# A two-layer long-convolution and MLP kernel: k, v, q and the spectrum swap moved in 4 KB rows, k and v loaded ahead of the second-stage tables, a new list of priorities

## The chip, the cores and the metric

The kernel runs on one core of one Trainium2 chip. The metric is the time of one execution on the device in microseconds (us); the time before is the median of three runs. The core has five engines with a program each: PE (TensorE, matmuls), DVE (VectorE), ACT (ScalarE), POOL (GpSimd) and SP (SyncE), which here only issues DMAs. Data lies in SBUF (128 partitions); PE writes to PSUM, from where ACT or DVE must copy ("evacuate") a result before PE can use the place again.

## The reference

```python
def _A_ref(q, k, v, shift_k, ssm_k, ssm_D):      # (1, 2048, 512) each
    ...                                          # k_shift: 4-tap causal filter of k along the sequence
    kv = k_shift * v
    L = 2 * S
    ...
    kv_f = rfft(kv padded to L); kf_f = rfft(ssm_k padded to L)
    y = irfft(kv_f * kf_f)[:, :S]                # a causal convolution over the sequence
    y = y + kv * ssm_D
    return q * y

x = A_q
x = x + _A_ref(layernorm(x), k, v, shift_k, ssm_k, ssm_D)
x = x + _B_ref(layernorm(x), w1, b1, w2, b2)     # layernorm, 512 -> 1376, gelu, 1376 -> 512
x = x + _A_ref(layernorm(x), k, v, ...)          # the same convolution output y, with the new x as q
x = x + _B_ref(layernorm(x), w1, b1, w2, b2)
```

All tensors are bf16. The convolution's y depends on k, v and the weights alone, so the kernel computes it once and uses it in both layers.

## The kernel before, in words

The program is straight-line: no loop runs on the chip. Python code declares operations, each with the memory that it reads and writes, its engine (or a choice of ACT and DVE for evacuations) and a planned length. A planner (`Prog.schedule`) then deals the operations out to the engines. It takes at each step the operation that can start first and breaks ties by a priority: the length of the work that hangs on the operation, plus a number for the operation's group from the table `BIAS`; `SHY` holds back DVE from taking an evacuation that ACT would do faster. The result is one fixed list per engine. `Prog.sync` adds the semaphore waits, and every engine works through its list in order. DMAs get a priority by the order in which they are declared, so SP's list follows the code's order where the data allow it.

The work, with the group names of the tables:

- **Loads.** SP issues the filter `ssm_k` (4 DMAs of 512 KB), `shift_k`, then eight 512 KB pieces of the table `tab_s2` (`tload`, L506) for the second transform stage, then two small DMAs with the last rows of the neighbour's k ("halo"), then k (one DMA, 128 partitions with 16 KB each), v (the same), small tables, biases.
- **ht, h1, h2: the filter's spectrum H.** Transposes (PE, L563), first stage (`stage1`, PE L580, 16 pairs of weight load and matmul to a group, each group evacuated by ACT L514 or DVE L515), second stage (`stage2`, PE L593, 16 groups of 8 pairs; needs `tab_s2`).
- **The spectrum swap.** The upper and lower 64 partitions of H are copied crosswise into a second buffer HS by four SBUF-to-SBUF DMAs (L498, `ar<-ar`) of 64 partitions with 16 KB each: two for the first half of the channels, two for the second. They wait for the last h2 evacuation, since each h2 group writes a stripe of every channel.
- **fir0 to fir3: the 4-tap filter of k, times v.** Blocks 0 and 1 of 128 channels go over PE (transposes L622, matmuls with diagonal weights L634, evacuated by DVE times v, L641). Blocks 2 and 3 are done on DVE alone, eight operations on 128x2048 each (L509).
- **x1_0 to x1_3: first transform stage of k*v** (`stage1` again, PE L580, 64 pairs for a channel block).
- **x2, i1, i2.** For each half of the channels (`PARTS`): second stage (`products`, PE L680, 8 groups of 16 pairs), evacuation, a DVE product with H and HS (L509, 128x2048), the first inverse stage (`inverse1`, PE L704); then `inverse2` (PE L760). These evacuations take 128x1024 each, nearly all on ACT.
- **T2, W1, q, W2** are loaded into the places of k and v, so SP issues them after fir and behind the swap.
- **The layers.** q and z: layer norms and gates on DVE and POOL; m1 and m2: the MLP's two products (PE L860 and L879), with gelu on ACT (L865) and the residual sum on DVE (L883). Transposes go over PE (L847) for the first blocks and over DMA later.

A "pair" below is one weight load (PEld) with its matmul (PE); PE's list holds 2248 of them. Up to the stage x2 they are numbered by adding up the counts of PE's rows.

Of the kernel before, what the change touches and what calls it, by code (L numbers as in the profile page):

```python
# [12 lines left out]
PE, ACT, DVE, POOL, SP = "tensor", "scalar", "vector", "gpsimd", "sync"  # L13
# [31 lines left out]
class Prog:  # L45
# [3 lines left out]

    G = 4  # L50
    LAT = 130.0
    BIAS = {'fir0': 55600, 'fir1': 5900, 'fir2': 62400, 'fir3': -169800, 'h1': 26100, 'h2': 31300, 'ht': 93000, 'i1_0': -56100, 'i1_64': 19100, 'i2_0': -72300, 'i2_64': 146700, 'm1': 113300, 'm2': -28100, 'q0': -4600, 'q1': -11900, 'q2': 28400, 'q3': -9200, 'q5': -46400, 'q6': -62400, 'q7': -55200, 'x1_0': 12800, 'x1_1': -24600, 'x1_2': -100, 'x1_3': 12900, 'x2_0': 193200, 'x2_64': 7000, 'z0': 8600, 'z1': -14300, 'z2': -51600, 'z3': -4800, 'z5': 11600, 'z6': 8700, 'z7': 49400}
    SHY = {'fir0': 1000, 'fir1': 300, 'h1': 0, 'h2': 210, 'ht': 1000, 'i1_0': 1000, 'i1_64': 0, 'i2_0': 3000, 'i2_64': 1000, 'x1_0': 150, 'x1_1': 2600, 'x1_2': 300, 'x1_3': 300, 'x2_0': 150, 'x2_64': 0, 'z0': 150, 'z1': 600}

    def __init__(self, nc):
        self.nc = nc
# [124 lines left out]
    def schedule(self):  # L181
# [9 lines left out]
        for o in reversed(ops):  # L191
# [19 lines left out]
        while done < n:  # L211
            best = None
            for e in free:
                te = max(free[e], 0.0)
                cand = None
                for o in ready[e]:
# [6 lines left out]
                    if new:  # L223
# [210 lines left out]
def bass_interleave_layers__ssm_conv_h3__mixer_channel_mlp__prompt_kernel(  # L434
        nc, A_q, A_k, A_v, A_shift_k, A_ssm_k, A_ssm_D, B_x, B_w1, B_b1, B_w2, B_b2, out):
    P = Prog(nc)
# [5 lines left out]
    def A(p0, n, off, *dims):  # L442
        return bass.AP(ar, p0 * AR + off, [[AR, n]] + [list(d) for d in dims])
# [12 lines left out]
    def dr(t, off, *dims):  # L456
        return bass.AP(t.tensor, off, [list(d) for d in dims])
# [39 lines left out]
    def dma(dst, src, nbytes, reads=(), prio=0.0, writes=None, eng=SP, rate=400.0):  # L497
        return P.op(eng, lambda e: e.dma_start(dst, src, allow_slow_non_contiguous=True), 550.0, reads=reads,  # L498
                    writes=[dst] if writes is None else writes, dma=True, nbytes=nbytes * 370 / rate, prio=prio)

    U16 = mybir.dt.uint16

    def tload(t, row, off, dst_off, n, eng=SP, prio=0.0):
        dst = A(0, 128, dst_off, [1, n])
        src = bass.AP(t, off, [[row, 128], [1, n]])
        return P.op(eng, lambda e: e.dma_start(dst.bitcast(U16), src), 450.0, writes=[dst], dma=True, nbytes=256 * n * .925, prio=prio)  # L506
# [32 lines left out]
    dma(A(16, 112, R_K + c0, [512, 3], [1, WDV]),
        dr(A_k, (16 * 15 + 13) * 512 + c0, [16 * 512, 112], [512, 3], [1, WDV]), 112 * 6 * WDV, writes=halo[1:2])  # L540
    dma(A(1, 15, R_K + c0, [512, 3], [1, WDV]),
        dr(A_k, 13 * 512 + c0, [16 * 512, 15], [512, 3], [1, WDV]), 15 * 6 * WDV, writes=halo[2:])
# [234 lines left out]
    def stats(sl, double, gate=()):  # L777
# [35 lines left out]
    for L in range(2):  # L813
        s0 = 0
        for n in (BLOCKS0, BLOCKS1)[L]:
# [15 lines left out]
            k = blk[0] % 2  # L831
            blk[0] += 1
            for i, s in enumerate(sl):
                z = ntmp()
                norm(s, mr[i], A(0, 128, z, [1, 512]))
                dst = A(0, 128, R_XT + k * 2048 + i * 128, [512, 4], [1, 128])
                if L or s >= 4:
                    zs = A(0, 128, z, [1, 512])
                    P.op(SP, lambda e, zs=zs, dst=dst: e.dma_start_transpose(dst, zs), 1300.0, reads=[zs], writes=[dst],
                         dma=True, nbytes=1 << 17)  # L840
                    continue
                tl = Tile(ptr)
                src = [A(0, 128, z + 128 * j, [1, 128]) for j in range(4)]
# [8 lines left out]
            for fc in range(11):  # L852
# [5 lines left out]
                def f(e, ins=ins, tl=tl, rows=rows, w=w):  # L858
# [4 lines left out]
                dst = A(0, rows, R_HT + k * 5632 + fc * 512, [1, w])  # L863
# [3 lines left out]
                    reads=[bias], writes=[dst], tile=tl)  # L867
            for i, s in enumerate(sl):
# [7 lines left out]
                for lo, hi in ((0, 4), (4, 8), (8, 11)):  # L876
                    def f(e, ins=ins, tl=tl, lo=lo, hi=hi):
# [45 lines left out]
```

## Time and profile before

| what | value |
|---|---|
| measured, median of 3 | 259.44 us (258.97 to 259.62) |
| the profiled execution | 257.8 us; its span on the chip 256.0 us |
| granted TensorE clock, mean | 0.98 |
| PE busy | 226.3 us, 88% |
| DVE busy | 175.9 us, 69% |
| ACT busy | 137.4 us, 54% |
| DMA traffic | 27.63 MB, queue q1 27.21 MB, queue q8 (instructions) 17 packets, 0.28 MB |

In the profile, an engine is followed by the line of the program, the operation, what it writes and reads (`ar` is SBUF, `ps` PSUM), shapes and counts. q1 is the queue of SP's DMAs, q8 the queue over which the engines' own program code comes in. "issue" is time in which an engine waited for nothing that the profile shows. The chain of waits is followed back from the end of the program: at each step to the work that released it.

The profiled execution is 1.6 us shorter than the median; the prediction's sum is made against the profiled one and the difference carried over.

### The profile page before, as it was taken

The page shows a single profiled execution, that of the slowest core. Times are in us where ns is not written, and L with a number is a line of the kernel's source. Part 1 is how long each engine was busy: PE and PEld are TensorE (multiplying, and loading weights), DVE is VectorE, ACT ScalarE, POOL GpSimd, SP SyncE. Part 2 cuts the span into 40 slices and gives each one's busy share as a digit, 9 for nine tenths or more (in the row PEclk, how much of TensorE's full clock was granted, in tenths as well). Part 3 has the DMA queues.
Part 4 walks back from the last instruction along what each step waited for, and adds up shares of the span by engine and source line. Part 5 has one row for each costly group of instructions (what it writes and reads, how often), then busy time and mean ns, then how long its engine had stood idle before and what let it go on. Part 6 is the DMA issues. An engine that isn't in the chain of part 4 may idle for free.

```text
span 256.0 us, 5259 instructions
## 1 busy us (share of the span) xinstructions
PE 226.3 (88%) x2233; PEld 147.3 (58%) x2248; DVE 175.9 (69%) x358; ACT 137.4 (54%) x189; POOL 29.9 (12%) x58
## 2 busy tenths in 40 slices
PE   2977688484869997999999999999999999999994
PEld 2966587383769995767654444444444444444441
DVE  0887699952999988892999939789697662102223
ACT  2478779481999888855621824705507445173000
POOL 1410000000000204212030110130203010000000
PEclk9999999975899999999999999999999999999999
DMA  6999918998990000022021220140224213110112
GB/s 248 358 375 366 416 24 164 246 205 265 382 337 5 5 0 0 3 41 44 0 51 32 44 41 0 26 60 0 42 41 64 63 20 62 44 41 37 45 41 82
DMA packets 23367, 27.63 MB, mean 108 GB/s; under 512 B 17233, under 2 KB 19248, under 8 KB 22448
## 3 DMA queue, kind: packets, MB, share of 16 engines
q1 hardware_dynamic: 23198, 27.21, 36.6%
q8 instruction: 17, 0.28, 0.4%
q10 hardware_dynamic: 146, 0.10, 0.2%
q14 instruction: 6, 0.05, 0.1%
HBM read 17.34 MB, written 2.10 MB: 76 GB/s over the span
## 4 chain that ended last, share of the span: by engine, by line
PE 67%; DVE 11%; DMA 7%; ACT 6%; issue 4%; SPq 4%
PE ps L879 29%; PE ps L860 28%; DVE ar L509 8%; DMA ar<-in_A_k_dram 7%; PE ps L704 6%; ACT ar L514 4%; SPq L498 3%; PE ps L580 3%; ACT ar L865 2%; SPq L506 1%; DVE ar L641 1%; DVE ar L515 1%; PE ps L680 1%; DVE ar L883 1%; PE ps L760 0%
## 5 line engine op out<-in xcount | busy, mean ns | idle before, releaser
L865 ACT ACTIVATE ar<-ps,sm 128x512 bf16<-128x512 f32 (+3 forms) x110 | 63.4, 601 | 72.4 <-PE ps L860 51.4
L514 ACT ACTIVATE ar<-ps 128x1024 bf16<-128x1024 f32 (+2 forms) x76 | 71.9, 1046 | 24.9 <-PE ps L580 17.5
L860 PE MATMUL ps<-ar 128*128 128x512 bf16 (+3 forms) x435 | 77.9, 336 | 1.3 <-ACT ar L514 1.1
L879 PE MATMUL ps<-ar 128*128 128x512 bf16 (+1 forms) x342 | 76.7, 379 | 0.5
L860 PEld LDWEIGHTS ps<-ar 128*128 128x128 bf16 (+1 forms) x440 | 43.7, 100 | 34.6 <-ACT ar L514 1.2
L509 DVE TENSOR_TENSOR ar<-ar 128x512 bf16<-128x512 bf16 (+2 forms) x104 | 60.8, 642 | 3.0 <-DMA ar<-in_A_k_dram 2.1
L879 PEld LDWEIGHTS ps<-ar 128*128 128x128 bf16 (+1 forms) x352 | 34.3, 98 | 40.7
L883 DVE TENSOR_TENSOR ar<-ar,ps 128x512 bf16<-128x512 bf16 x32 | 21.1, 683 | 50.3 <-PE ps L879 50.3
L788 DVE BATCH_NORM_STATS2 sm<-ar 128x6 f32<-128x512 bf16 (+1 forms) x68 | 41.1, 644 | 0.0
L515 DVE CAST ar<-ps 128x1024 bf16<-128x1024 f32 x18 | 21.3, 1217 | 10.6 <-PE ps L680 5.1
L580 PE MATMUL ps<-ar 128*64 128x128 bf16 x512 | 18.5, 233 | 10.9 <-issue 8.9
L803 DVE TENSOR_SCALAR ar<-ar,sm 128x512 bf16<-128x512 bf16 x64 | 22.7, 403 | 6.3 <-POOL sm L796 4.8
L580 PEld LDWEIGHTS ps<-ar 128*64 128x64 bf16 x512 | 16.6, 119 | 12.6 <-issue 9.4
L796 POOL TENSOR_TENSOR sm<-sm 128x4 f32<-128x4 f32 (+1 forms) x20 | 17.9, 897 | 1.7
L794 POOL TENSOR_SCALAR sm<-sm 128x4 f32<-128x4 f32 (+1 forms) x20 | 4.3, 217 | 107.0 <-DVE sm L790 106.9
L704 PE MATMUL ps<-ar 128*128 128x128 bf16 x256 | 14.9, 220 | 1.8 <-DVE ar L509 1.5
L704 PEld LDWEIGHTS ps<-ar 128*128 128x128 bf16 x256 | 14.6, 114 | 2.0 <-DVE ar L509 1.6
L680 PE MATMUL ps<-ar 128*128 128x64 bf16 x256 | 10.6, 207 | 1.4 <-ACT ar L514 1.4
L680 PEld LDWEIGHTS ps<-ar 128*128 128x128 bf16 x256 | 9.7, 107 | 2.3 <-ACT ar L514 2.1
L515 DVE COPY ar<-ps 128x2048 bf16<-128x2048 bf16 x4 | 4.8, 1225 | 7.3 <-PE ps L563 7.3
L563 PE MATMUL ps<-ar 128*128 128x128 bf16 x64 | 5.5, 261 | 4.8 <-DMA ar<-in_A_ssm_k_dram 4.8
L593 PE MATMUL ps<-ar 128*128 128x128 bf16 x128 | 8.1, 219 | 1.6 <-ACT ar L514 1.2
(24 smaller groups left out, 71.2 us busy)
## 6 DMA issues: line engine op xcount, KB each, us to landing
ar<-tab_s SPq DMA_DIRECT2D x8, 512.0 KB, 12.7
ar<-ar SPq DMA_DIRECT2D x4, 1024.0 KB, 14.7
ar<-in_A_ssm_k_dram SPq DMA_DIRECT2D x4, 512.0 KB, 5.4
ar<-in_A_k_dram SPq DMA_DIRECT2D x1, 2048.0 KB, 17.2
ar<-in_A_v_dram SPq DMA_DIRECT2D x1, 2048.0 KB, 21.7
ar<-in_A_q_dram SPq DMA_DIRECT2D x2, 1024.0 KB, 16.4
out_dram<-ar SPq DMA_DIRECT2D x8, 256.0 KB, 2.0
ar<-in_B_w_dram SPq DMA_DIRECT2D x1, 1376.0 KB, 19.5
```

The lines of the kernel that those rows point to most:

```text
L509: return P.op(eng, lambda e: e.tensor_tensor(o, a, b, op), dur, reads=[a, b] + list(more), writes=[o])
L514: return e.activation(dst, src(), AF.Copy)
L515: return e.tensor_copy(dst, src())
L580: r = e.matmul(Q(tl, 64 * ri, 64, i * 128, [1, 128]), w, m, start=True, stop=True)
L680: r = e.matmul(Q(tl, 0, 128, i * pitch, [1, n]), w, m, start=True, stop=True)
L704: r = e.matmul(Q(tl, 0, 128, i * 128, [1, 128]), w, m, start=q == 0, stop=q == 1)
L788: P.op(DVE, lambda e, sj=sj, x=x: e.bn_stats(sj, x), 80.0 + 1.18 * w, reads=[x], writes=[sj], gate=gate)
L803: P.op(DVE, lambda e: e.tensor_scalar(o, x, m, r, ALU.subtract, ALU.mult), 405.0, reads=[x, m, r], writes=[o])
L860: r = e.matmul(Q(tl, 0, rows, 0, [1, w]), a, m, start=dk == 0, stop=dk == 3)
L865: P.op(ACT, lambda e, dst=dst, tl=tl, rows=rows, bias=bias, w=w: e.activation(dst, Q(tl, 0, rows, 0, [1, w]), AF.Gelu_apprx_tanh, bias=bia ...
L879: r = e.matmul(Q(tl, 0, 128, 0, [1, 512]), ins[fc][0], ins[fc][1], start=fc == 0, stop=fc == 10)
L883: P.op(DVE, lambda e, x=x, tl=tl: e.tensor_tensor(x, x, Q(tl, 0, 128, 0, [1, 512]), ALU.add), 690.0, reads=[x], writes=[x], tile=tl)
```

## The change

```diff
-    BIAS = {'fir0': 55600, 'fir1': 5900, 'fir2': 62400, ...}
-    SHY = {'fir0': 1000, 'fir1': 300, 'h1': 0, ...}
+    BIAS = {'fir0': 83800, 'fir1': -43400, 'fir2': 54600, ...}
+    SHY = {'fir0': 1000, 'fir1': 0, 'h1': 150, ...}
...
+LOADS = ("k", "v", 0, 1, 2, 3, 4, 5, 6, 7)
...
-    for j in range(8):
-        tload(t_s2, 128 * 128, j * 2048, R_S2 + j * 2048, 2048)
-    dma(... halo of k, two DMAs ...)
-    dma(A(0, 128, R_K + 1536, [1, 8192]), dr(A_k, 0, [16 * 512, 128], [1, 8192]), 1 << 21)
-    dma(A(0, 128, R_V, [1, 8192]), dr(A_v, 0, [16 * 512, 128], [1, 8192]), 1 << 21)
+    def load(step):
+        if step == "k":
+            dma(... halo of k, the same two DMAs ...)
+            for j in range(4):
+                dma(A(0, 128, R_K + 1536 + 2048 * j, [1, 2048]), dr(A_k, 2048 * j, [16 * 512, 128], [1, 2048]), 1 << 19)
+        elif step == "v":
+            for j in range(4):
+                dma(A(0, 128, R_V + 2048 * j, [1, 2048]), dr(A_v, 2048 * j, [16 * 512, 128], [1, 2048]), 1 << 19)
+        else:
+            tload(t_s2, 128 * 128, step * 2048, R_S2 + step * 2048, 2048)
+    for step in LOADS:
+        load(step)
...
     for d0, n in PARTS:
         for g in range(2):
-            src, dst = [A(64 * p, 64, r + 128 * d0, [1, 128 * n]) for p, r in ((g, R_H), (1 - g, R_HS))]
-            dma(dst, src, n << 14, reads=[src], rate=217.0)
+            for c in range(0, 128 * n, 2048):
+                src, dst = [A(64 * p, 64, r + 128 * d0 + c, [1, 2048]) for p, r in ((g, R_H), (1 - g, R_HS))]
+                dma(dst, src, 1 << 18, reads=[src], rate=210.0)
...
-    for g in range(2):
-        dma(A(0, 128, R_X + 4096 * g, [1, 4096]), dr(A_q, 4096 * g, [16 * 512, 128], [1, 4096]), 1 << 20)
+    for g in range(4):
+        dma(A(0, 128, R_X + 2048 * g, [1, 2048]), dr(A_q, 2048 * g, [16 * 512, 128], [1, 2048]), 1 << 19)
```

The planner's rates for DMAs change with it (`rate`, 400 to 370 for loads, and a factor in `tload`); they change only what the planner assumes. The bytes moved are the same: k, v and q go in 4 KB rows (k and v 16 KB before, q 8 KB before), the swap in 16 DMAs of 64 rows of 4 KB in place of 4 DMAs of 64 rows of 16 KB.

On SP, at the program's start, before (`tab_s` is the second-stage table, `in_A_k_dram` first the two halo DMAs and then k):

```order
L498 DMA ar<-in_A_ssm_k_dram 128x2048 x4
L498 DMA ar<-in_A_shift_k_dram 128x2048
L506 DMA ar<-tab_s 128x2048 x8
L498 DMA ar<-in_A_k_dram 112x3x256
L498 DMA ar<-in_A_k_dram 15x3x256
L498 DMA ar<-in_A_k_dram 128x8192
L498 DMA ar<-in_A_v_dram 128x8192
L506 DMA ar<-tab_small 128x256
L498 DMA ar<-in_B_b_dram 128x10x1
L498 DMA ar<-in_B_b_dram 96x1
L498 DMA ar<-ar 64x8192 x4
L506 DMA ar<-tab_small 128x4096
```

And of the change at the same place (lines are one higher):

```order
L499 DMA ar<-in_A_ssm_k_dram 128x2048 x4
L499 DMA ar<-in_A_shift_k_dram 128x2048
L499 DMA ar<-in_A_k_dram 112x3x256
L499 DMA ar<-in_A_k_dram 15x3x256
L499 DMA ar<-in_A_k_dram 128x2048 x4
L499 DMA ar<-in_A_v_dram 128x2048 x4
L507 DMA ar<-tab_s 128x2048 x8
L507 DMA ar<-tab_small 128x256
L499 DMA ar<-in_B_b_dram 128x10x1
L499 DMA ar<-in_B_b_dram 96x1
L499 DMA ar<-ar 64x2048 x16
L507 DMA ar<-tab_small 128x4096
```

The eight table pieces moved from ahead of k and v to behind them; the swap's four DMAs became sixteen at the same place.

On PE, from the end of the transposes (80 pairs are done) to the stage x2, before (L580 first h1, later x1; L593 h2; L622 and L634 fir; L680 x2):

```order
L580 MATMUL ps<-ar 64x128 x240
L593 MATMUL ps<-ar 128x128 x88
L622 MATMUL ps<-ar 128x128 x16
L593 MATMUL ps<-ar 128x128 x24
L634 MATMUL ps<-ar 128x128 x64
L593 MATMUL ps<-ar 128x128 x16
L622 MATMUL ps<-ar 128x128 x16
L580 MATMUL ps<-ar 64x128 x64
L634 MATMUL ps<-ar 128x128 x64
L580 MATMUL ps<-ar 64x128 x192
L680 MATMUL ps<-ar 128x64 x208
```

And of the change (L590, L603, L633, L645 and L691 are the same five lines of code):

```order
L590 MATMUL ps<-ar 64x128 x160
L633 MATMUL ps<-ar 128x128 x16
L590 MATMUL ps<-ar 64x128 x64
L645 MATMUL ps<-ar 128x128 x64
L590 MATMUL ps<-ar 64x128 x16
L633 MATMUL ps<-ar 128x128 x16
L603 MATMUL ps<-ar 128x128 x128
L590 MATMUL ps<-ar 64x128 x64
L645 MATMUL ps<-ar 128x128 x64
L590 MATMUL ps<-ar 64x128 x176
L691 MATMUL ps<-ar 128x64 x80
L590 MATMUL ps<-ar 64x128 x16
```

Both transposes of k and the first filter block moved ahead of h2; h2 became one run of 128 pairs; the last x1 group moved behind the first five groups of x2. Behind the last row shown L691 goes on. Added up from 80, the first seven rows of the change and the first seven of before both end at pair 544 with the same work done: h1, h2, both transposes and one filter block.

On DVE, from the last h1 evacuations to the end of fir, before (L515 CAST 128x8x32x4 is an h2 evacuation, L509 fir, L641 a filter block times v):

```order
L515 CAST ar<-ps 128x8x32x4 x4
L509 TENSOR_TENSOR ar<-ar 128x2048 x6
L641 TENSOR_TENSOR ar<-ps,ar 128x32x32
L509 TENSOR_TENSOR ar<-ar 128x2048
L641 TENSOR_TENSOR ar<-ps,ar 128x32x32
L509 TENSOR_TENSOR ar<-ar 128x2048 x4
L641 TENSOR_TENSOR ar<-ps,ar 128x32x32
L509 TENSOR_TENSOR ar<-ar 128x2048
L641 TENSOR_TENSOR ar<-ps,ar 128x32x32
L509 TENSOR_TENSOR ar<-ar 128x2048 x4
```

And of the change (the lines L516, L510 and L652 are the same three), up to the last h2 evacuation:

```order
L510 TENSOR_TENSOR ar<-ar 128x2048
L516 COPY ar<-ps 128x16x128
L510 TENSOR_TENSOR ar<-ar 128x2048 x3
L652 TENSOR_TENSOR ar<-ps,ar 128x32x32 x2
L510 TENSOR_TENSOR ar<-ar 128x2048 x2
L516 CAST ar<-ps 128x8x32x4
L510 TENSOR_TENSOR ar<-ar 128x2048
L516 CAST ar<-ps 128x8x32x4
L510 TENSOR_TENSOR ar<-ar 128x2048
L516 CAST ar<-ps 128x8x32x4 x4
```

Behind these stand four operations of L510, two of L652 and four of L510. Six h2 evacuations and one copy of transposed k now stand between the fir operations; before, the h2 evacuations stood ahead of all of them.

More of the change, by code (lines that the diff above doesn't have):

```diff
@@ L51 @@
     LAT = 130.0
-    BIAS = {'fir0': 55600, 'fir1': 5900, 'fir2': 62400, 'fir3': -169800, 'h1': 26100, 'h2': 31300, 'ht': 93000, 'i1_0': -56100, 'i1_64': 19100, 'i2_0': -72300, 'i2_64': 146700, 'm1': 113300, 'm2': -28100, 'q0': -4600, 'q1': -11900, 'q2': 28400, 'q3': -9200, 'q5': -46400, 'q6': -62400, 'q7': -55200, 'x1_0': 12800, 'x1_1': -24600, 'x1_2': -100, 'x1_3': 12900, 'x2_0': 193200, 'x2_64': 7000, 'z0': 8600, 'z1': -14300, 'z2': -51600, 'z3': -4800, 'z5': 11600, 'z6': 8700, 'z7': 49400}
-    SHY = {'fir0': 1000, 'fir1': 300, 'h1': 0, 'h2': 210, 'ht': 1000, 'i1_0': 1000, 'i1_64': 0, 'i2_0': 3000, 'i2_64': 1000, 'x1_0': 150, 'x1_1': 2600, 'x1_2': 300, 'x1_3': 300, 'x2_0': 150, 'x2_64': 0, 'z0': 150, 'z1': 600}
+    BIAS = {'fir0': 83800, 'fir1': -43400, 'fir2': 54600, 'fir3': -219300, 'h1': 39000, 'h2': 18300, 'ht': 155000, 'i1_0': -114900, 'i1_64': 24300, 'i2_0': -179500, 'i2_64': 54600, 'm1': 74700, 'm2': -45000, 'q0': 3500, 'q1': -4700, 'q2': 145200, 'q3': -6300, 'q5': -57000, 'q6': -80400, 'q7': -74600, 'x1_0': -53700, 'x1_1': 64300, 'x1_2': -7500, 'x1_3': 21300, 'x2_0': 210400, 'x2_64': 68700, 'z0': 9300, 'z1': -23300, 'z2': -64900, 'z3': 38400, 'z5': -30700, 'z6': -33300, 'z7': -12500}
+    SHY = {'fir0': 1000, 'fir1': 0, 'h1': 150, 'h2': 0, 'ht': 3000, 'i1_0': 0, 'i1_64': 0, 'i2_0': 150, 'i2_64': 600, 'x1_0': 770, 'x1_1': 300, 'x1_2': 150, 'x1_3': 1000, 'x2_0': 600, 'x2_64': 0, 'z0': 600, 'z1': 600}
     def __init__(self, nc):
@@ L495, in bass_interleave_layers__ssm_conv_h3__mixer_channel_mlp__prompt_kernel, with dma @@
     t_s2 = nc.inline_tensor(_bf(S2), name="tab_s2")
-    def dma(dst, src, nbytes, reads=(), prio=0.0, writes=None, eng=SP, rate=400.0):
+    def dma(dst, src, nbytes, reads=(), prio=0.0, writes=None, eng=SP, rate=370.0):
         return P.op(eng, lambda e: e.dma_start(dst, src, allow_slow_non_contiguous=True), 550.0, reads=reads,
@@ L505, in tload @@
         src = bass.AP(t, off, [[row, 128], [1, n]])
-        return P.op(eng, lambda e: e.dma_start(dst.bitcast(U16), src), 450.0, writes=[dst], dma=True, nbytes=256 * n * .925, prio=prio)
+        return P.op(eng, lambda e: e.dma_start(dst.bitcast(U16), src), 450.0, writes=[dst], dma=True, nbytes=256 * n, prio=prio)
     def tt(o, a, b, op, dur, eng=DVE, more=()):
@@ L536, in bass_interleave_layers__ssm_conv_h3__mixer_channel_mlp__prompt_kernel @@
         P.op(ACT, lambda e, o=o, s=s: e.activation(o, s, AF.Copy), 600.0, reads=[s], writes=[o])
-    for j in range(8):
-        tload(t_s2, 128 * 128, j * 2048, R_S2 + j * 2048, 2048)
[L539 to L542, printed above, removed]
-    dma(A(0, 128, R_K + 1536, [1, 8192]), dr(A_k, 0, [16 * 512, 128], [1, 8192]), 1 << 21)
-    dma(A(0, 128, R_V, [1, 8192]), dr(A_v, 0, [16 * 512, 128], [1, 8192]), 1 << 21)
+    def load(step):
+        if step == "k":
+            dma(A(16, 112, R_K + c0, [512, 3], [1, WDV]),
+                dr(A_k, (16 * 15 + 13) * 512 + c0, [16 * 512, 112], [512, 3], [1, WDV]), 112 * 6 * WDV, writes=halo[1:2])
+            dma(A(1, 15, R_K + c0, [512, 3], [1, WDV]),
+                dr(A_k, 13 * 512 + c0, [16 * 512, 15], [512, 3], [1, WDV]), 15 * 6 * WDV, writes=halo[2:])
+            for j in range(4):
[7 more added lines that the diff above has]
+        load(step)
     for i in range(NPE):
```

## Prediction

> **What bounds the kernel now.** I read the chain of waits first, whole and then in order of time.
>
> ```profile
> span 256.0 us, 5259 instructions
> PE 67%; DVE 11%; DMA 7%; ACT 6%; issue 4%; SPq 4%
> ```
>
> ```profile
> 12.22 17.24 DMA ar<-in_A_k_dram
> ...
> 47.92 3.33 issue
> 51.25 4.24 PE ps L580 x87
> ...
> 57.21 4.14 issue
> 61.35 0.64 PE ps L580 x8
> 61.98 0.98 PE ps L680 x16
> ```
>
> Up to 29.5 us the chain is loads with k at their end, then the filter of k on DVE, then x1 on PE with two holes of 3.33 and 4.14 us in which PE waits for nothing that the profile shows. Next the stages (columns: busy time and instructions of PE, PEld, DVE, ACT, POOL; PE's clock, DMA share, GB/s):
>
> ```profile
> 29.48:52.80 23.32, 17.30 (x363) 16.23 (x365) 23.19 (x20) 16.13 (x16) 1.24 (x2) 0.98 0.74 175
> 57.21:61.35 4.14, 0.00 (x2) 0.00 (x1) 0.66 (x1) 0.10 (x1) 0.00 (x0) 0.70 0.91 198
> 64.25:82.42 18.17, 15.01 (x334) 14.04 (x332) 18.17 (x16) 17.83 (x20) 1.04 (x2) 0.96 0.69 249
> 99.81:252.13 152.32, 151.52 (x783) 78.33 (x799) 95.75 (x256) 64.33 (x112) 19.25 (x34) 1.00 0.17 37
> ```
>
> DVE is full from 29.48 to 52.80 with fir (20 operations). In the second hole DVE and ACT stand still too. From 64.25 to 82.42 DVE (16 products, 1.136 us each) and ACT are both full; from 99.81 PE is, with the MLPs. So a gain has to come from ahead of x2, and nearly all of it survives.
>
> **What the holes are.** The PE timeline, weight loads:
>
> ```profile
> 16.97 2.96 PEld L580 LDWEIGHTS ps<-ar 128*64 128x64 bf16 x98 [1.64 <-issue]
> 21.29 1.64 PEld L593 LDWEIGHTS ps<-ar 128*128 128x128 bf16 x29 [1.36 <-ACT ar L514]
> 39.96 1.81 PEld L580 LDWEIGHTS ps<-ar 128*64 128x64 bf16 x64 [1.37 <-DVE ar L641]
> 51.25 5.00 PEld L580 LDWEIGHTS ps<-ar 128*64 128x64 bf16 x119 [3.49 <-issue]
> 56.80 0.31 PEld L580 LDWEIGHTS ps<-ar 128*64 128x64 bf16 x9 [0.54 <-DVE ar L515]
> 66.75 1.53 PEld L680 LDWEIGHTS ps<-ar 128*128 128x128 bf16 x48 [0.29 <-ACT ar L514]
> ```
>
> Between the holes lie 119 + 9 = 128 weight loads and their matmuls: 256 instructions. A packet of q8 has 16 KB (0.28 MB in 17, table above). So PE's code comes in blocks of 256 instructions, and the holes are blocks that came late, at pairs 729 and 857; counting back by 128 the borders are 601, 473, some 348 and 222 (hole at 16.97), forward 985. PE entered block 601 as the 57th pair of the third row, at 41.7. The DMA view of what followed each entry:
>
> ```profile
> DMA packets 423, 1.46 MB, mean 396 GB/s; under 512 B 42, under 2 KB 71, under 8 KB 423
> q1 hardware_dynamic: 423, 1.46, 101.0%
> q8 instruction: 1, 0.02, 5.8%
> ...
> DMA packets 101, 1.39 MB, mean 202 GB/s; under 512 B 16, under 2 KB 16, under 8 KB 16
> q1 hardware_dynamic: 101, 1.39, 95.2%
> q8 instruction: 1, 0.02, 5.1%
> ...
> DMA packets 102, 1.41 MB, mean 196 GB/s; under 512 B 16, under 2 KB 16, under 8 KB 16
> q1 hardware_dynamic: 102, 1.41, 93.4%
> q8 instruction: 1, 0.02, 5.6%
> ```
>
> The first two rows of each three are the time from entry to fetch (16.97:20.65, 41.7:48.6, 51.25:58.45), where every packet is q1's; the third is the next 1.2 to 1.6 us, which hold the code packet. So, as I read it, the next block is asked for on entering a block, and its packet waits until about 1.4 MB of other traffic has passed: 3.7 us under loads from HBM, 6.9 to 7.2 us under the swap, which runs at half the rate. PE goes on 2.7 to 2.9 us after the packet's start (48.6 to 51.25, 58.45 to 61.35).
>
> **The change part by part.**
>
> *Loads.* The bytes stay. The windows of the start:
>
> ```profile
> 0.00:10.00 10.00, 5.16 (x69) 5.01 (x70) 3.02 (x3) 1.50 (x2) 2.13 (x10) 1.00 0.78 284
> 10.00:20.00 10.00, 8.42 (x255) 7.67 (x252) 8.60 (x8) 8.35 (x10) 3.18 (x4) 1.00 1.01 377
> 20.00:30.00 10.00, 6.05 (x100) 5.41 (x97) 6.54 (x7) 7.78 (x9) 0.00 (x0) 1.00 1.04 386
> ```
>
> Ahead of k now lie 2.6 MB and 0.2 MB of halo, k has 2.1 MB: 4.9 MB, of which 2.8 are moved by 10 us and the rest takes 5.5 us at 377 GB/s. The same reckoning puts k's last byte of before at 26.5, 3 us ahead of the chain's 29.46; I take 2 of these, since one code packet lies ahead of k where there were two: k at 17.5 instead of 29.46 (up to 18.5), v some 5.5 us later, the table's last piece (11.2 MB in all) at about 34 instead of 22. The tables, in 4 KB rows, ran at 377 GB/s and k and v, in 16 KB rows, at 386, so I give the rows themselves nothing (the ends: 2% of 4 MB each way, 0.2 us).
>
> *DVE's fir* starts at about 17.5 but shares DVE with seven evacuations: 27 operations at 23.32/20 = 1.17 us are 31.5 us, plus 1 us for waits on PE and on table pieces: 50.0, instead of 52.8.
>
> *The swap* waits for the last h2 evacuation, DVE's 17th of these: 17.5 + 17 x 1.17 + 0.8 = 38.2, against the 38.82 of before (row below). This is the chosen middle: the tables alone would let it go at 35.5, and DVE held up by each filter block at 39.5. Transfer as before, 4.2 MB at 202 GB/s, 20.8 us; its end near 60.
>
> ```profile
> 38.82 6.17 SPq L498 DMA_DIRECT2D ar<-ar  x4
> L498 SPq DMA_DIRECT2D ar<-ar x4: 547/1424/2648, 38.8 to 42.7; - x4
> L506 SPq DMA_DIRECT2D ar<-tab_s x8: 431/439/586, 3.1 to 6.7; - x8
> 56.45 1.72 SPq L498 DMA_DIRECT2D ar<-in_A_q_dram  x2
> ar<-in_A_q_dram SPq DMA_DIRECT2D x2, 1024.0 KB, 16.4
> 82.42 1.27 DVE L788 BATCH_NORM_STATS2 sm<-ar 128x6 f32<-128x512 bf16 x2
> ```
>
> *Sixteen issues* for four: by the table's 0.44 us 7 us, by the swap's median 1.42 us 23 us, by its longest 2.65 us 42 us. Beside 20.8 us of transfer the first costs nothing and the last binds. I take the first, since the table's rows are the same 4 KB and were also issued into a full queue. T2, W1, q and W2 queue behind. Of these q is read first, at 82.42, and landed at about 56.45 + 16.4 = 72.9, so there are 9 us of cover.
>
> The Trainium skill, "DMA: Bandwidth & Descriptors" (Rules for kernel authors), asks for at least 1 MiB in a DMA and speaks against 256 KB pieces. By it the swap would lose rate; the table's eight 512 KB pieces at 377 GB/s do not bear that out where DMAs queue behind each other.
>
> *PE's blocks.* The borders stay at pairs 601, 729, 857, 985; the code under them moves. Pair 601 is now in the x1 group just behind h2, which PE reaches as h2's last evacuations free PSUM: 38.5 to 39.5, within a microsecond of the swap's issue instead of 2.9 us behind it (41.7 against 38.82). Its request then meets an empty queue, and the **first hole goes** (3.33 us). Pair 729 is reached at about 45.2 (two products L652 end by 38.2 + 6 x 1.17). It asks for block 857 in mid-swap: 45.2 + 7.1 + 2.8 = 55.1. PE meanwhile ends x1 some 1.7 us behind fir, at 51.7, does half a group of x2 and **waits 3 us** at pair 857. There block 985 is asked for: 5.1 us of swap (1.0 MB) and 1.1 us of loads, then 2.8: 64.1.
>
> *The sum.* Pair 985 is the 121st of x2 in both programs. Before it was issued at 66.75 + 25/48 x 1.53 = 67.55 (96 of x2's pairs lie ahead of that row). From there the work is the same: 67.55 - 64.1 = **3.5 us**. Unknown are the race at pair 601, the middle for the swap's start (up to 1 us) and the queue wait of 4 KB rows in the swap.
>
> Behind it PE's list changes only in counts of one or two pairs (33 and 41 for 34 and 40 of L879); at 0.38 us a matmul that is nothing on a full PE. The profiled run becomes 254.3; with the same distance to the median, 259.44 - 3.5 = **255.9**.
>
> **The rivals.**
>
> *The code waits get short.* If a code packet waits for a number of rows or DMAs rather than for bytes, a swap in 4 KB rows cuts its wait to a quarter, and both holes go. Then x2 starts at 51.7 and pair 985 comes 121 pairs later, at 0.046 us each (61.98 to 67.55), at 57.3 to 58: over 9 us gained, of which q's cover and ACT, full from then on, leave about 8: **251.4**. For it: SP may keep fewer bytes queued. Against it: 1.46 MB passed in 4 KB rows and 1.39 and 1.41 in 16 KB rows.
>
> The Trainium skill, "DMA: Bandwidth & Descriptors" (Queues, rings and completion order), says that a DMA engine changes between queues only after a whole packet, some 9 to 17 descriptors; by that rule this rival is right. The traffic above goes by bytes and is against it.
>
> *The race is lost.* Pair 601's request falls behind the swap's start: block 729 at 39 + 7.1 + 2.8 = 48.9, block 857 at 58.8, block 985 (0.3 MB of swap, 1.1 MB of loads) at 66: gain 1.5, **257.9**.
>
> *Slower: the issue binds.* If SP needs for each of the 16 issues the mean of the two long ones before (about 2.45 us), the swap lands at 38.2 + 39.2 + 1.5 = 79. The second half's products waited before until 64.25 + 8 x 1.136 = 73.3: **5.7 us lost, 265.1**. It decides from (73.3 - 38.2 - 1.5)/16 = 2.1 us an issue.
>
> *No change.* The h2 evacuations behind fir operations start the swap and x1 late by 3 us more: **259.4**.
>
> **How the numbers follow.** Forecast 0.46 (254.4 to 257.2 by its own unknowns), short waits 0.24, lost race 0.12, issue-bound 0.09, no change 0.09. The likeliest is 255.9. A range from 250.9 to 259.8 takes in the first three and most of the last. A run of this kernel tells 0.3% (0.8 us) from no change; faster by more: 0.46 + 0.24 + 0.10 = 0.80, within 0.09, slower 0.11.
>
> **What would show it.** In the changed profile: DVE's first fir operation at 17 to 18; the swap's first issue at 37 to 39.5; no hole of PE near 45 to 48; a hole of about 3 us ending near 55 with L691 behind it and one of 2 to 4 us ending near 64; in the DMA view 1.4 MB between entry and code packet. No holes at all says short waits; a hole at pair 729 the lost race; SP busy with the swap past 60 says that the issue binds. I am wrong at the root if the holes move without regard to the 128-pair borders.

## The result, and the profile after

| what | before | after |
|---|---|---|
| measured, median | 259.53 us (258.97 to 260.18) | 250.24 us (248.85 to 252.08) |
| ratio | | 0.9645 [0.9573, 0.9718] |
| the profiled execution, its span | 257.8, 256.0 us | 252.08, 250.0 us |
| pair 601, 729, 857 | 41.50, 51.26, 61.35 us | 40.31, 46.67, 54.41 us |
| pair 985 | 67.55 us | 59.22 us |
| first pair of i2, of m1 | 90.22, 99.81 us | 82.46, 92.05 us |
| last end | 255.97 us | 249.94 us |

The change gains 9.3 us; the forecast was 3.5 (255.9), and the time lies just under the range (250.9). The profiled execution of before lay 1.6 us under its kernel's median of 259.44, that of after 1.8 above its own, so the traces show 6.0 us between the spans, of 7.8 that PE had gained at m1.

The chain of waits of the changed kernel, first its shares by engine, from the page.

```profile
span 250.0 us, 5306 instructions
PE 75%; ACT 7%; SPq 6%; DVE 5%; DMA 5%; issue 1%; DVEq 0%
```

"issue", 4% before, is 1%, and SPq and DMA take its place. The chain in order of time (start, length, what):

```profile
16.60 1.51 issue
...
40.92 1.89 SPq L499
...
55.54 7.95 DMA ar<-ar
63.48 0.04 DVEq L370
63.52 2.19 DVE ar L510 x2
...
69.79 12.89 PE ps L715 x224
```

The holes of 3.33 and 4.14 us are not on it; of PE's code waits the one at 16.60 is left. From 40 us the chain is the swap: SP's issues one after the other, then the last piece's landing at 63.5. PE's weight loads in the timeline (start, length, what, count; in brackets the idle time before and what ended it):

```profile
46.47 1.37 PEld L590 LDWEIGHTS ps<-ar 128*64 128x64 bf16 x48 [0.21 <-DVE ar L652]
...
51.28 2.53 PEld L590 LDWEIGHTS ps<-ar 128*64 128x64 bf16 x48 [1.67 <-DVE ar L510]
53.99 2.38 PEld L691 LDWEIGHTS ps<-ar 128*128 128x128 bf16 x64 [0.17 <-issue]
...
58.97 0.52 PEld L691 LDWEIGHTS ps<-ar 128*128 128x128 bf16 x16 [0.16 <-ACT ar L515]
```

Pair 729 is the ninth of the first row; pair 857 the ninth of L691's 64 and pair 985 the ninth of the last row, and neither waits for anything. What PE waits for here are the engines DVE and ACT. The DMA view from PE's entry of block 729 to just after its code packet began:

```profile
DMA packets 115, 0.38 MB, mean 227 GB/s; under 512 B 25, under 2 KB 25, under 8 KB 114
q1 hardware_dynamic: 114, 0.36, 105.9%
q8 instruction: 1, 0.02, 5.1%
...
ar<-ar SPq DMA_DIRECT2D x2, 256.0 KB, 6.5
```

0.36 MB of q1 passed where the forecast had 1.4: 1.68 us instead of 7.1. The last row has the median from issue to landing of a swap DMA, 6.5 us; in the page of before it is 14.7. From the swap's first row to its last (40.9 to 62.1 us) the DMA engines moved 213 GB/s, so a piece of 256 KB takes about 1.2 us and at most some five pieces, 1.4 MB, lie between an issue and its landing. Before there were about three of 1 MB (14.7 us at 217 GB/s).

### The profile page after: what moved, and what is told of

Same layout as the page of the kernel before. It is cut to its first block, busy times and chain, and to the rows that moved or that the text cites. A ratio compares the mean times of both kernels' runs of the same rounds, so it can differ in the third digit from the quotient of the medians.

```text
span 250.0 us, 5306 instructions
## 1 busy us (share of the span) xinstructions
PE 229.5 (92%) x2248; PEld 147.2 (59%) x2248; DVE 175.7 (70%) x358; ACT 136.6 (55%) x189; POOL 29.7 (12%) x58
## 4 chain that ended last, share of the span: by engine, by line
PE 75%; ACT 7%; SPq 6%; DVE 5%; DMA 5%; issue 1%; DVEq 0%
PE ps L871 31%; PE ps L890 30%; ACT ar L515 6%; SPq L499 6%; PE ps L715 6%; DMA ar<-ar 3%; DVE ar L510 3%; PE ps L573 2%; PE ps L590 2%; DMA ar<-in_A_ssm_k_dram 2%; PE ps L645 2%; DVE ar L516 1%; DVE ar L894 1%; DVE ar L652 0%; ACT ar L537 0%
## 5 line engine op out<-in xcount | busy, mean ns | idle before, releaser
L876 ACT ACTIVATE ar<-ps,sm 128x512 bf16<-128x512 f32 (+3 forms) x110 | 63.5, 601 | 73.9 <-PE ps L871 53.0
L871 PE MATMUL ps<-ar 128*128 128x512 bf16 (+3 forms) x440 | 79.8, 342 | 1.1 <-ACT ar L515 1.1
L515 ACT ACTIVATE ar<-ps 128x1024 bf16<-128x1024 f32 (+2 forms) x76 | 70.9, 1036 | 18.1 <-PE ps L590 15.0
L890 PE MATMUL ps<-ar 128*128 128x512 bf16 (+1 forms) x352 | 78.1, 379 | 0.0
L871 PEld LDWEIGHTS ps<-ar 128*128 128x128 bf16 (+1 forms) x440 | 44.5, 102 | 35.4 <-ACT ar L515 1.2
L510 DVE TENSOR_TENSOR ar<-ar 128x512 bf16<-128x512 bf16 (+2 forms) x104 | 61.0, 643 | 0.8 <-ACT ar L515 0.7
L890 PEld LDWEIGHTS ps<-ar 128*128 128x128 bf16 (+1 forms) x352 | 34.4, 98 | 40.6
L590 PE MATMUL ps<-ar 128*64 128x128 bf16 x512 | 18.9, 230 | 4.3 <-issue 1.5
L516 DVE CAST ar<-ps 128x1024 bf16<-128x1024 f32 x17 | 20.2, 1220 | 2.2 <-PE ps L590 1.7
L590 PEld LDWEIGHTS ps<-ar 128*64 128x64 bf16 x512 | 16.1, 116 | 6.7 <-issue 1.9
L807 POOL TENSOR_TENSOR sm<-sm 128x4 f32<-128x4 f32 (+1 forms) x20 | 18.6, 931 | 1.7
L715 PE MATMUL ps<-ar 128*128 128x128 bf16 x256 | 14.9, 220 | 1.8 <-DVE ar L510 1.6
L715 PEld LDWEIGHTS ps<-ar 128*128 128x128 bf16 x256 | 14.5, 114 | 2.1 <-DVE ar L510 1.7
L516 DVE COPY ar<-ps 128x2048 bf16<-128x2048 bf16 x5 | 6.2, 1232 | 9.3 <-PE ps L573 8.3
L691 PE MATMUL ps<-ar 128*128 128x64 bf16 x256 | 9.8, 195 | 1.8 <-ACT ar L515 1.6
L573 PE MATMUL ps<-ar 128*128 128x128 bf16 x64 | 6.6, 291 | 4.9 <-DMA ar<-in_A_ssm_k_dram 4.9
L691 PEld LDWEIGHTS ps<-ar 128*128 128x128 bf16 x256 | 8.4, 99 | 3.2 <-ACT ar L515 2.5
L603 PE MATMUL ps<-ar 128*128 128x128 bf16 x128 | 8.4, 220 | 1.8 <-ACT ar L515 0.9
## 6 DMA issues: line engine op xcount, KB each, us to landing
ar<-ar SPq DMA_DIRECT2D x16, 256.0 KB, 6.5
out_dram<-ar SPq DMA_DIRECT2D x8, 256.0 KB, 2.0
```

The source lines that it names most:

```text
L515: return e.activation(dst, src(), AF.Copy)
L516: return e.tensor_copy(dst, src())
L590: r = e.matmul(Q(tl, 64 * ri, 64, i * 128, [1, 128]), w, m, start=True, stop=True)
L715: r = e.matmul(Q(tl, 0, 128, i * 128, [1, 128]), w, m, start=q == 0, stop=q == 1)
L807: P.op(POOL, lambda e: e.tensor_tensor(r, v, hf, ALU.pow), 1020.0, reads=[v, hf], writes=[r])
L871: r = e.matmul(Q(tl, 0, rows, 0, [1, w]), a, m, start=dk == 0, stop=dk == 3)
```

## The experiments

Two numbers serve all of them. **The code wait** is the time from PE's entry of a block (pair 729 or 857, counted from PE's rows as in the prediction) to the start of q8's next packet; "none" says that the packet had started by then. **Landing** is the page's median from the issue of a swap DMA to its landing, which tells how much is queued. In the first group all engines' lists are the same but SP's. "Span" is of the profiled execution. The ratio is to runs of before taken beside each kernel, whose medians were 258.34 to 259.93 us.

| kernel | swap | landing, us | code wait at 729, 857, us | pair 985 | span | median, us | ratio to before |
|---|---|---|---|---|---|---|---|
| *lists of after* | | | | | | | |
| e1 | 4 x 1 MB, rows 16 KB | 14.6 | 7.99, 6.24 | 64.97 | 252.6 | 253.45 | 0.9784 [0.972, 0.9847] |
| e8 | 4 x 1 MB, rows 4 KB | 14.5 | 7.62, 6.77 | 65.62 | 253.0 | 254.19 | 0.9774 [0.9693, 0.9856] |
| e4 | 8 x 512 KB, rows 4 KB | 10.2 | 2.08, 2.88 | 57.82 | 246.9 | 249.85 | 0.9665 [0.9584, 0.9746] |
| e3 | 16 x 256 KB, rows 16 KB | 6.5 | 2.68, 2.77 | 58.55 | 247.9 | 250.32 | 0.9661 [0.9598, 0.9723] |
| after | 16 x 256 KB, rows 4 KB | 6.5 | 1.68, 1.35 | 59.22 | 250.0 | 250.24 | 0.9645 [0.9573, 0.9718] |
| e10 (after again) | the same | 6.7 | 2.03, 2.44 | 57.80 | 248.1 | 249.13 | 0.9618 [0.9565, 0.9671] |
| e9 | 32 x 128 KB, rows 2 KB | 2.6 | 1.50, none | 58.89 | 249.1 | 249.50 | 0.9595 [0.9508, 0.9682] |
| e6 | as after; k, v, q in long rows | 6.4 | 1.57, 0.99 | 57.69 | 246.7 | 249.64 | 0.9599 [0.9523, 0.9675] |
| e11 | as e9; k, v, q in long rows | 2.4 | 0.82, none | 58.30 | 248.4 | 249.56 | 0.9622 [0.9562, 0.9683] |
| *other lists* | | | | | | | |
| before | 4 x 1 MB, rows 16 KB | 14.7 | 7.27, 3.70 | 67.55 | 256.0 | 259.53 | 1 |
| e2 (before's) | 16 x 256 KB, rows 4 KB | 6.6 | 2.28, 2.28 | 60.69 | 250.5 | 251.85 | 0.9723 [0.9665, 0.9781] |
| e5 (tables first) | 16 x 256 KB, rows 4 KB | 6.5 | 2.14, 3.52 | 62.96 | 256.0 | 257.86 | 0.9959 [0.9928, 0.9991] |
| e7 (old priorities) | 16 x 256 KB, rows 4 KB | 11.7 | 6.61, 6.31 | 68.27 | 256.5 | 257.75 | 0.9933 [0.9893, 0.9973] |

Before has its two long waits at pairs 601 (7.16 us) and 729; at 857 its swap is nearly over.

### Which part removed the holes: e1 and e2

e1 is the changed kernel with the old swap:

```diff
-            for c in range(0, 128 * n, 2048):
-                src, dst = [A(64 * p, 64, r + 128 * d0 + c, [1, 2048]) for p, r in ((g, R_H), (1 - g, R_HS))]
-                dma(dst, src, 1 << 18, reads=[src], rate=210.0)
+            src, dst = [A(64 * p, 64, r + 128 * d0, [1, 128 * n]) for p, r in ((g, R_H), (1 - g, R_HS))]
+            dma(dst, src, n << 14, reads=[src], rate=210.0)
```

> The changed kernel with the swap alone put back to 4 DMAs of 64 rows of 16 KB; the lists of PE, DVE, ACT and POOL are the same as the changed kernel's. Theory 'rows' (while the swap runs, a code packet waits until some 5 to 6 rows of its DMA engine have gone, whatever their size: 7 us in 16 KB rows, 1.5 to 1.8 us in 4 KB rows): the code packet that the changed kernel fetched 1.7 us after pair 729 comes 7 us after it, PE stands 2 us at pair 857 and 3 to 4 us at pair 985; 255 to 256.5 us. Theory 'bytes queued' (it waits for the bytes that SP has put in the queue, and SP keeps fewer there with 256 KB DMAs): the same. Theory 'order' (the holes went because the new lists put other code under the block borders, the swap's form is nothing): 250.2 us, no holes.

PE's timeline of e1:

```profile
53.00 0.45 PEld L690 LDWEIGHTS ps<-ar 128*128 128x128 bf16 x8 [0.17 <-issue]
56.28 3.29 PEld L690 LDWEIGHTS ps<-ar 128*128 128x128 bf16 x72 [2.83 <-issue]
...
60.58 1.22 PEld L690 LDWEIGHTS ps<-ar 128*128 128x128 bf16 x40
64.94 4.74 PEld L690 LDWEIGHTS ps<-ar 128*128 128x128 bf16 x88 [3.14 <-issue]
```

This is the program that the prediction described: holes of 2.83 and 3.14 us right at pairs 857 and 985 (its eight pairs of L690, then a stop), ending at 56.3 and 64.9 (forecast 55.1 and 64.1), and i2 at 86.82, 3.4 us earlier than before (forecast 3.5). Its median lies further off: 253.45 us, under the 255 to 256.5 expected and 4.9 under that of before beside it (258.34). The holes come back with the swap alone, under the new lists. e2 is the reverse, the kernel before with the new swap, the diff's lines turned round:

> The kernel before with the swap alone in 16 DMAs of 64 rows of 4 KB; the lists of the other engines as before. 'rows' and 'bytes queued': the code packets come 1.5 to 2 us after pairs 601 and 729, the holes of 3.33 and 4.14 us go, x2 starts some 6 us earlier; 252.5 to 254 us. 'order': the holes stay, 259.5 us.

Its PE timeline in the swap:

```profile
47.01 1.43 PEld L580 LDWEIGHTS ps<-ar 128*64 128x64 bf16 x48 [0.39 <-ACT ar L514]
...
54.31 0.82 PEld L580 LDWEIGHTS ps<-ar 128*64 128x64 bf16 x16 [0.25 <-DVE ar L515]
55.30 2.07 PEld L681 LDWEIGHTS ps<-ar 128*128 128x128 bf16 x48 [0.17 <-issue]
```

Pair 729 lies in the first of these rows and pair 857 in the second, and both rows run through: the holes of 3.33 and 4.14 us are gone, with the old lists. The waits, 2.28 us, are a little longer and the time, 251.85 us, a little shorter than expected. So with either of these lists the form of the swap decides the holes, and it alone brings 2.8% where the whole change brings 3.6 to 3.8%.

### Rows or bytes queued: e3, e4, e8, e9

The new swap differs from the old in the row (4 KB for 16) and in the DMA (256 KB for 1 MB). e3 has small DMAs of long rows, by taking every fourth partition:

```diff
-            for c in range(0, 128 * n, 2048):
-                src, dst = [A(64 * p, 64, r + 128 * d0 + c, [1, 2048]) for ...]
+            for c in range(4):
+                src, dst = [bass.AP(ar, (64 * p + c) * AR + r + 128 * d0, [[4 * AR, 16], [1, 128 * n]]) for ...]
...
```

> The changed kernel with the swap in 16 DMAs of 256 KB as it has them, but each of 16 rows of 16 KB (every fourth partition) in place of 64 rows of 4 KB; all other lists the same. 'rows': the waits of 7 us and both holes return, 255 to 256.5 us. 'bytes queued': as many bytes in a DMA and as many DMAs as the changed kernel, so waits of 1.5 to 2 us, no holes, 250.2 us. 'order': 250.2 us.

e8 has large DMAs of short rows; the four rows of a partition lie in falling order, so they don't join:

```diff
-            for c in range(0, 128 * n, 2048):
-                src, dst = [A(64 * p, 64, r + 128 * d0 + c, [1, 2048]) for ...]
-                dma(dst, src, 1 << 18, ...)
+            src, dst = [A(64 * p, 64, r + 128 * d0 + 6144, [-2048, 4], [1, 2048]) for ...]
+            dma(dst, src, n << 14, ...)
```

> The changed kernel with its swap in 4 DMAs of 1 MB, each row of a partition cut into four rows of 4 KB that lie in falling order (so that they don't join into 16 KB); every engine's list is the same. It completes the square of row size by DMA size. 'Bytes queued' (the code packet waits for what SP has put in the queue, about three DMAs' worth): waits of 6 to 8 us for the blocks asked for at pairs 729 and 857, two holes of about 3 us, pair 985 near 65 us, 253.5 us, as with four DMAs of 16 KB rows (253.45). 'Rows' (it waits for a number of rows): waits of 1.3 to 1.7 us, no holes, pair 985 near 59, 250.3 us. A mixture would give waits near 4 us and some 251.5 us.

The DMA view of e8 from entry of pair 729 to its code packet:

```profile
DMA packets 413, 1.64 MB, mean 215 GB/s; under 512 B 16, under 2 KB 16, under 8 KB 412
q1 hardware_dynamic: 412, 1.62, 102.3%
q8 instruction: 1, 0.02, 1.1%
```

and of e1 over the same stretch:

```profile
DMA packets 126, 1.80 MB, mean 226 GB/s; under 512 B 16, under 2 KB 16, under 8 KB 16
q1 hardware_dynamic: 126, 1.80, 106.0%
```

The code waited for 396 rows of 4 KB in the one and 110 rows of 16 KB in the other, 7.62 and 7.99 us. The size of the row is worth next to nothing, while behind the same 4 KB rows in 256 KB DMAs the code waited 4 to 6 us less (after and e10). PE's timeline of e8 has the holes at the same pairs:

```profile
56.38 3.19 PEld L691 LDWEIGHTS ps<-ar 128*128 128x128 bf16 x72 [2.53 <-issue]
...
65.59 4.74 PEld L691 LDWEIGHTS ps<-ar 128*128 128x128 bf16 x88 [3.72 <-issue]
```

and that of e3, with the long rows, only a short one:

```profile
54.08 1.65 PEld L693 LDWEIGHTS ps<-ar 128*128 128x128 bf16 x48 [0.40 <-DVE ar L516]
...
58.52 0.77 PEld L693 LDWEIGHTS ps<-ar 128*128 128x128 bf16 x24 [0.56 <-issue]
```

e3's waits, 2.68 and 2.77 us, are still some 1 us above the 1.5 to 2 that "bytes queued" expected.

e4 takes two 4 KB rows of each partition into a DMA (`[4096, 2], [1, 2048]`, 512 KB), e9 1024 elements for 2048 (128 KB):

> The changed kernel with the swap in 8 DMAs of 512 KB, 128 rows of 4 KB each (every second 4 KB piece); all other lists the same. 'rows': the wait for a code packet in the swap stays 1.5 to 1.8 us, 250.2 us. 'bytes queued': the wait doubles, to 3 to 4 us, with a hole under 1 us; 250.2 to 251 us. 'order': 250.2 us. If SP's issues bind the changed kernel's swap (16.97 us for 16 issues), the swap here ends earlier; if the DMA engines do, it ends at the same time.

> The changed kernel with its swap in 32 DMAs of 128 KB (2 KB rows). 'Bytes queued': with three DMAs ahead of it the code packet waits 1 us or less at pairs 729 and 857; there is no hole left in the swap for that to take, so the time stays at 250 us (249.5 to 250.8). 'Rows': the same by another road, 0.4 to 0.9 us. If instead SP's cost of an issue binds (0.44 us each would be 14 us, 1.25 us each 40 us), the swap's last packet lands past 70 us instead of 62.4 and the kernel takes 254 to 258 us.

No wait in either made a hole over 1 us, and neither time can be told from that of after. But the waits don't follow the size of the DMA as "bytes queued" had it: twice the piece was to double them, to 3 to 4 us, and e4 has 2.08 and 2.88. e9's "1 us or less" was missed once: 1.50 at pair 729. In e9 SP's row and the DMA view from 40.6 to 64.2 us read:

```profile
39.48 24.60 SPq L499 DMA_DIRECT2D ar<-ar  x32
```

```profile
q1 hardware_dynamic: 2401, 3.95, 77.7%
```

Here the issue does set the swap's pace: 0.77 us each, and q1 keeps the engines 78% busy, where they were full in after (row below). The swap's last row ends at 65.7 us for 62.4 in after. The times show no cost of that, but the swap itself is longer: smaller pieces no longer come free.

### The loads' rows: e6, e11, and after again

e6 puts k and v back into one DMA each (besides the halo's two) and q into two:

```diff
-            for j in range(4):
-                dma(A(0, 128, R_K + 1536 + 2048 * j, [1, 2048]), dr(A_k, 2048 * j, [16 * 512, 128], [1, 2048]), 1 << 19)
+            dma(A(0, 128, R_K + 1536, [1, 8192]), dr(A_k, 0, [16 * 512, 128], [1, 8192]), 1 << 21)
...
-    for g in range(4):
-        dma(A(0, 128, R_X + 2048 * g, [1, 2048]), dr(A_q, 2048 * g, ...), 1 << 19)
+    for g in range(2):
+        dma(A(0, 128, R_X + 4096 * g, [1, 4096]), dr(A_q, 4096 * g, ...), 1 << 20)
```

> The changed kernel with k and v each in one 2 MB DMA of 16 KB rows and q in two of 8 KB rows, as before the change; every engine's list is the same. If the row of the loads is worth nothing, as the prediction took it: the first filter operation of DVE at 17.7 us and 250.3 us (249.5 to 251.2). If four smaller DMAs bring k or q earlier, or shorten the wait for PE's code under the loads: first filter operation 0.5 to 1 us later, waits for code under the loads 1 to 3 us longer, 251.5 to 253 us.

The first filter operation of DVE in e6:

```profile
17.68 1.22 DVE L510 TENSOR_TENSOR ar<-ar 128x2048 bf16<-128x2048 bf16 x1 [0.64 <-DMA ar<-in_A_k_dram]
```

17.68 us, as in after (17.70), and the time is no longer: the rows of the loads do nothing that these runs show. e11 joins e6 and e9, with after beside them:

> The changed kernel with k, v and q in few long-row DMAs (249.64 us alone) and the swap in 32 DMAs of 128 KB (249.50 alone); every engine's list is the same. 'Both were the scatter of 250.3': 249.3 to 250.5 us, no better than the changed kernel beside it. 'Each is worth its own 0.6 to 0.8 us': 248.5 to 249.2 us.

> The changed kernel once more, unedited, beside the two others of this job and with more runs: 250.2 us, from 249.5 to 251. If its gain over the forecast (255.9) came from the chip of the first runs and not from the kernel, nearer to 256 us.

249.56 and 249.13 us: all of these agree, and no version was found that is clearly better than after.

### The loads' order and the priorities: e5 and e7

e5 keeps the new priorities and puts the tables first again:

```diff
-LOADS = ("k", "v", 0, 1, 2, 3, 4, 5, 6, 7)
+LOADS = (0, 1, 2, 3, 4, 5, 6, 7, "k", "v")
```

> The changed kernel with the eight table pieces ahead of k and v, as before the change; its rows, its swap and its priorities stay, and the planner's lists follow the later loads. 'Short code waits are the gain, the order of loads some 1.5 us': DVE's first long run of filter operations near 29 us, no holes in the swap, 251.5 to 253 us, near the kernel before with only the swap changed (251.85). 'The order is worth what the prediction gave it (3 us)': 253 to 254 us. 'The order is worth nothing': 250.3 us.

All three were wrong: 257.86 us, 6 us above e2, which has the same order of loads and differs in the priorities, the planner's transfer rates and the rows of the loads. The chain of waits of e5 shows a part of the reason, and DVE's timeline the same place:

```profile
57.11 10.62 DMA ar<-in_A_q_dram
67.75 1.29 DVE sm L799 x2
```

```profile
67.75 1.29 DVE L799 BATCH_NORM_STATS2 sm<-ar 128x6 f32<-128x512 bf16 x2 [1.68 <-DMA ar<-in_A_q_dram]
69.61 1.21 DVE L516 CAST ar<-ps 128x1024 bf16<-128x1024 f32 x1
```

With late loads the new priorities put q's layer norm ahead of an evacuation on DVE's list, where it waits for q with PE behind it. e7 keeps the new loads and takes the old `BIAS` and `SHY` (those two lines of the diff turned round):

> The changed kernel with the priorities of before; its rows, its swap in 16 DMAs and its loads (k and v first) stay, and the planner's lists follow. DVE then does 15 of its first filter operations ahead of most of h2's evacuations, so the swap is issued after some 22 operations of 1.17 us from 17.7, near 43 to 44 us, 4 us later than 39.7. 'The priorities are half of the change': pair 985 about 4 us later than 59.2, 253.5 to 255 us. 'Short code waits are all that counts': within 1 us of 250.3, as the filters' own end near 51 us sets x2 whatever the order of the swap.

257.75 us, 3 us above the higher range. SP's timeline tells what was not foreseen:

```profile
39.93 0.39 SPq L499 DMA_DIRECT2D ar<-in_B_w_dram  x1
43.09 18.12 SPq L499 DMA_DIRECT2D ar<-ar  x16
61.26 3.22 SPq L499 DMA_DIRECT2D ar<-in_A_q_dram  x4
```

T2, W1 and W2 now go ahead of the swap, and their last packets end at 50.9 us. The swap's pieces pile up behind them: its packets begin at 47.7, by when SP was at its sixth issue, and landing takes 11.7 us for 6.5. With it the code wait is long again, in the same 256 KB pieces. From the entry of pair 729:

```profile
DMA packets 414, 1.33 MB, mean 203 GB/s; under 512 B 80, under 2 KB 93, under 8 KB 414
q1 hardware_dynamic: 414, 1.33, 104.3%
```

and PE's timeline:

```profile
59.03 0.45 PEld L590 LDWEIGHTS ps<-ar 128*64 128x64 bf16 x8 [5.22 <-issue]
```

A hole of 5.22 us, and the next wait, from pair 857, is 6.31 us, 8 us after the last packet of T2, W1 and W2. This miss speaks for the queue: the pieces are those of after, and more of them lie ahead of the code packet. (The lists differ too, so it is no test of the queue alone.)

## Why the prediction was wrong, step by step

- **What the holes are** (PE's code in blocks of 256 instructions, the next asked for at entry): right. e1 has its holes at pairs 857 and 985 as counted.
- **Loads:** right. k at 17.5 forecast, DVE at 17.70; no gain from the rows (e6).
- **DVE's fir** to 50.0, x2 at 51.7: 51.23 (49.97 + 1.26, the last filter operation in DVE's timeline) and 53.99 (PE's, above).

```profile
17.70 1.22 DVE L510 TENSOR_TENSOR ar<-ar 128x2048 bf16<-128x2048 bf16 x1
...
49.97 1.26 DVE L510 TENSOR_TENSOR ar<-ar 128x2048 bf16<-128x2048 bf16 x1
...
54.10 2.52 DVE L516 CAST ar<-ps 128x1024 bf16<-128x1024 f32 x2 [1.73 <-PE ps L590]
56.54 18.25 DVE L510 TENSOR_TENSOR ar<-ar 128x2048 bf16<-128x2048 bf16 x16
```

  The operations of x2 (last row) ran through from 56.54, and the chain above has one of them released by the swap's last landing at 63.48. An earlier start would have met that landing, so x2's late start cost little.

- **The swap's start:** 38.2 forecast, 39.70 measured, 0.2 us past the upper bound of 39.5 (in e10 38.9).
- **Sixteen issues:** 16.97 us, 1.06 each, neither the 0.44 taken nor the 2.45 of the rival, and under its limit of 2.1. SP's row and the DMA view from 40.6 to 62.5:

```profile
39.70 16.97 SPq L499 DMA_DIRECT2D ar<-ar  x16
...
60.17 1.77 SPq L499 DMA_DIRECT2D ar<-in_A_q_dram  x4
```

```profile
DMA packets 1331, 4.64 MB, mean 212 GB/s; under 512 B 256, under 2 KB 256, under 8 KB 1280
q1 hardware_dynamic: 1328, 4.59, 101.1%
```

  The engines are full at 212 GB/s, so SP only follows them. The Trainium skill, "DMA: Bandwidth & Descriptors" (Rules for kernel authors), asks for at least 1 MiB in a DMA. This case doesn't bear that out for 256 KB pieces: from the swap's first row to its last the engines moved 213 GB/s in after, and 215 in e8 with the same rows in DMAs of 1 MB. A loss shows in e9's 128 KB pieces (173).
- **The race at pair 601:** won, as forecast; entered at 40.31, its packet 0.50 us later, the hole of 3.33 us gone.
- **"It asks for block 857 in mid-swap: 45.2 + 7.1 + 2.8 = 55.1", and "5.1 us of swap" for block 985: this step failed.** The packets came after 1.68 and 1.35 us. The 7.1 us came from "its packet waits until about 1.4 MB of other traffic has passed", a figure read from three places, where DMAs of 512 KB to 2 MB lay behind one another. It was a property of those queues, and I carried it as a constant into a program that changes the queue. Where the queue is like that again, so is the figure: from the entry of pair 985 in after, with T2 and W1 queued behind the last of the swap, 1.35 MB passed in 5.1 us before the packet. PE needed that block only after it had come, so no hole shows. The same step had the answer as a rival ("SP may keep fewer bytes queued", 251.4 us, 0.24). The argument set against it (1.46 MB passed in 4 KB rows too) compared rows; those loads were DMAs of 512 KB and 2 MB behind one another. e8 and e3 separate the two.
- **The rival's own reckoning** nearly held: pair 985 "at 57.3 to 58" was 59.22 (57.80 in e10); "over 9 us gained, of which q's cover and ACT, full from then on, leave about 8" was 8.33 at pair 985 and 7.76 at i2. The limits it names, from the windows of after (columns as in the prediction):

```profile
56.50:74.70 18.20, 14.55 (x326) 13.35 (x327) 18.20 (x17) 17.86 (x20) 1.04 (x2) 1.00 1.03 324
...
92.05:95.60 3.55, 3.54 (x18) 2.47 (x19) 2.69 (x9) 1.42 (x3) 1.75 (x4) 0.52 0.00 0
```

  In the first, DVE is busy 18.20 of 18.20 us and ACT 17.86. That fits e1, whose pair 985 is 5.75 us later than after's but whose i2 only 4.4. q's pieces land from 71.80 to 75.67 and DVE reads it from 74.70 on, without a wait: the cover is used up. It was also less than the 9 us of the prediction, which took the median landing; before, the last of q landed at 74.32, 8.1 us ahead of q's first use.
- **"From there the work is the same":** nearly. From m1 to the end after takes 157.9 us, before 156.2. The second row above shows where: the granted clock is 0.52 for 3.5 us at m1's start, 1.7 us of work. It is 1.00 there in before. e10 has the same dip and ends at 248.0, as PE reached m1 at 90.14.
- **The change of priorities,** costed as moved code only: with the loads it is worth what is left, 251.85 us (e2) less 249.13 to 250.24, some 2 us. The intervals of the ratios overlap a little; beside e2, e3 and e4, with the lists of after, took 250.32 and 249.85. Alone, the new priorities (e5) and the new loads (e7) each cost 6 us against e2.

What stays open: how much of a queue passes ahead of a code packet. With landings of 6.4 to 10.2 us the waits in mid-swap are 1.0 to 2.9 us, with 11.7 to 14.7 they are 6.2 to 8.0 (e5's 3.52 falls on the swap's end, with the loads behind it). That is no fixed share, and whether bytes, DMAs or something inside the DMA engines set it, these runs don't tell. Nor was it tried whether the swap on another engine's queue would leave the code packets free.

## What to carry to other kernels

A wait read from a profile holds for the queue in which it was read: before carrying it into a program with other DMAs, ask how much was queued there and what will be queued now. In this straight-line code with its long list on PE, large DMAs stacked on one queue delayed the engine's own code; 256 KB pieces cost the transfer no rate here and took the holes away. And change orders and priorities together: the new loads and the new priorities were worth some 2 us as a pair, and either one without the other cost 6.

## What the runs showed of the hardware

- In mid-swap a code packet waited at most 2.9 us behind swap DMAs of 128 to 512 KB, 6.2 to 8.0 us behind those of 1 MB, whatever the row, and 6.3 to 6.6 us behind 256 KB pieces that had piled up (e7). The Trainium skill, "DMA: Bandwidth & Descriptors" (Queues, rings and completion order), has an engine change queues after a packet of some 9 to 17 descriptors. Here 110 rows of 16 KB or 396 of 4 KB passed in about the same time (7 and 25 for each of the 16 engines), so the count of rows did not decide. Whether a row is one descriptor the traces don't show.
- In the swap of after SP's issues took 0.54 to 0.64 us, but for one of 1.89, while the queue was short, and then mostly 1.0 to 1.3 us, about the transfer time of 256 KB (1.2 us). As I read it, SP is held back by what is queued. What it counts is not shown, and it isn't bytes alone: at the start of after SP issued 15 DMAs with 7.0 MB in 7.2 us, 0.48 us each, while only 2.2 MB were moved.
- Holes of PE go with a lower granted clock: over 50 to 66 us its mean was 0.68 in before, 0.72 in e1 and 0.73 in e8, and 0.89 in after and 0.95 in e3, which have none that long. Which of the two brings the other is not shown.
